# A convolution kernel's seam: the last step's spectra kept on chip, the other rows reloaded a step earlier, the inverse products moved ahead of the mixing's transposes

## The chip, the cores and the metric

One core of a Trainium2 chip runs the kernel; the others are idle. The metric is the device time of one execution in microseconds: 677.84 us, the median of 3 runs (677.25 to 677.91). TensorE is written PE, VectorE DVE, ScalarE ACT, GpSimd POOL, and SP is the engine that only issues transfers.

## The reference

Two halves, each modulated by a condition vector `c` (shift, scale and gate are 512 wide each), over a sequence of 2048 rows of 512 channels:

```python
# half A: a long convolution per channel, through the Fourier transform
P = jnp.exp(logdA[:, :, None] * l[None, None, :])
K = jnp.einsum("dn,dnl,dn->dl", Cc, P, dB).real
Kf, Uf = rfft2(pad(K)), rfft2(pad(u))
y = irfft2(Uf * Kf)[..., :L] + u * Dskip
x = x + ga * y                                   # u = layernorm(x) * (1 + ca) + sa
# half B: on h = layernorm(x) * (1 + cb) + sb
m  = gelu(layernorm(h) @ w1)                     # then shifted by +1, -1, +2, -2 rows by quarter
x1 = h + shifted(m) @ w2
x  = x + gb * (x1 + gelu(layernorm(x1) @ w3) @ w4)
```

## The kernel before, in words

All is fp32; half B's products are split into high and low parts and done as three products. Up to about 205 us the kernel builds the convolution's taps and the input's first transform. Then come the spectra, and then half B.

**The spectral loop** (`steps`, 16 of them) covers two channel halves `jh` of 256 channels, each in 8 steps `kc`. A step does, on PE, `spectrum_k` (64 products, taps, from the buffer `VK[jh]` with the tables `T2` and `T3`) and `spectrum_u` (the input, with the table `TU`); on ACT the copies `us`; on DVE `multiply`, which leaves `zc0` and `zc1`. `back` turns these with the table `Gm` (tile name FK): four products of 64 columns into two banks `pz`, which ACT evicts to `z`. POOL stores `z` to the DRAM scratch `ZT[jh]`; in the very last step SP and ACT each store half. The loop is skewed: `back` of step n-1 stands in pass n, `spectrum_u` of step n+1 too.

**The inverse** needs, for each output block, rows of all 8 steps, in another order: `load_inv` reads `ZT[jh]` back in 8 chunks of 128 rows by 4 x 256, and `inv_half(jh, g, i)` does 8 products of 32 columns (`FI` times a chunk) into a bank; DVE adds it to `X2`, the sequence in row blocks (tile name KX). `g` is one of four groups of four blocks, `i` a pair in it. The first half's inverse (`jh` 0) runs in passes 14 and 15 and around the end of the loop. The second half's can only start when the last step's rows have been stored and loaded.

**Behind the seam** the mixing runs through groups 7, 0, 1, 2, ... of 256 rows: `first_stats`, `mix_mod1`, `mix_mod2` (DVE with POOL for the roots), `mix_norm` (ACT), `transposed` (PE, 8 transposes to `pT0` and `pT1`), `parts_of` (ACT makes `nh`, DVE the residual `nl`), `mix_half` (PE products with `W1h` and `W1l`, ACT's gelu `go`, a store to `GD`). The closures `a31`, `a00`, `a30`, `a01`, `a10`, `a11`, `a20` and `a21` are DVE's adds of the second half's eight inverse tiles. `keep(n)` issues n products that nobody reads, into `pT0`.

**What sets the order.** Everything here is in a manual schedule: each engine runs its instructions in the order of the program text, and only waits on semaphores. Tiles that share memory make an instruction wait for the last user. Transfers from SP and ACT take turns on eight semaphores; a transfer waits until the eighth before it has landed. So an instruction that is late delays all that stands behind it on its engine.

Of the kernel before, what the change touches and what calls it, by code (L numbers as in the profile page):

```python
# [24 lines left out]
NXC = 16 * NX0 + 64 * NX1  # L25


def shape_constants():
# [19 lines left out]
    Gm = np.tile(np.concatenate([cs, cs], 1), (2, 1))  # L48
    sg = np.array([1.0, -1.0])[:, None]
    th = 2 * np.pi * (k1[:, None, None, None] + .5) * (sg * be[:, None, None] + 64 * q) / 4096  # L50
    FI = np.stack([np.cos(th), -sg * np.sin(th), -np.sin(th), -sg * np.cos(th)]) * (2 / 4096)
    eye = np.eye(16)
# [18 lines left out]
    for e in range(16):  # L71
# [9 lines left out]
        FI=FI.reshape(128, 32 * 64), C0=C0, C1=C1, CE=CE, PA=PA.reshape(128, 512), PB=PB.reshape(128, 2048), ID=np.eye(128)).items()}  # L81
# [28 lines left out]
def dram(t, off, ap):  # L110
    return bass.AP(tensor=t.tensor, offset=t.offset + off, ap=ap)


def body(ctx, tc, A):
# [534 lines left out]
    T3 = s2.tile([128, 32, 64], F32, name="T3", bufs=1)  # L649

# [37 lines left out]
    def back(jh, kc):  # L688
        zc = zcs.pop((jh, kc))
        z = s2.tile([128, 4, 256], F32, name="z", bufs=3)  # L690
        o = [psa.tile([128, 2, 256], F32, name="pz") for kk in range(2)]
        for n in range(2):
            for kk in range(2):
                r = slice(kk * 64, kk * 64 + 64)
                T.matmul(o[kk][n * 64:n * 64 + 64], Gm[r, n], zc[n][r], start=True, stop=True, skip_group_check=True)  # L695

        def store(q, a, b):
            for n in range(2):
                q.dma_start(dram(ZT[jh], n * 16384 + (kc * 4 + a) * 256, [[32768, 32], [8192, 2], [1, (b - a) * 256]]),
                            z[n * 64:n * 64 + 64, a:b].rearrange("p k d -> p (k d)"))  # L700

        last = (jh, kc) == (1, 7)
        for kk in range(2):
            act(z[:, 2 * kk:2 * kk + 2], o[kk])
            if last:
                store((Y, S)[kk], 2 * kk, 2 * kk + 2)
        if not last:
            store(P, 0, 4)

    def load_inv(jh, k, i=None, q=Y):  # L710
        if (jh, k) not in zis:
            zis[jh, k] = block() if jh or k in (1, 2, 5, 6) else zip_.tile([128, 4, 256], F32, name="zi")
        a, n = (0, 4) if i is None else (2 * i, 2)
        q.dma_start(zis[jh, k][:, a:a + n], dram(ZT[jh], (k * 4 + a) * 32768, [[256, 128], [32768, n], [1, 256]]))

    def load_x(g):
        P.dma_start(X2[:, g * 4:g * 4 + 4].rearrange("p b d -> p (b d)"), A["x"][g])

    def inv_half(jh, g, i, pl, name):
        p = pl.tile([128, 2, 256], F32, name=name)  # L720
        for e in range(2):
            b = g * 4 + i * 2 + e
            for bp, (c, sg) in enumerate(((31 - b, 1), (15 - b, 1), (b, 0), (16 + b, 0))):
                T.matmul(p[bp * 32:bp * 32 + 32, e], FI[:, c, sg], zis[jh, c // 4][:, c % 4],
                         start=True, stop=True, skip_group_check=True)
        x = X2[:, g * 4 + i * 2:g * 4 + i * 2 + 2, jh * 256:jh * 256 + 256]
        return lambda: V.tensor_add(x, p, x)
# [365 lines left out]
    with tc.manual_schedule():  # L1093
# [13 lines left out]
        for n, st in enumerate(steps):  # L1107
# [26 lines left out]
            if n == 14:  # L1134
                inverse(0, 0)
                for b in range(4):
                    half_stat(b, 0)
                w2r = [block().rearrange("p (a c) b -> p a (c b)", a=2) for i in range(2)]
                for i in range(2):
                    Y.dma_start(w2r[i], A["w2"][256 * i:256 * i + 256].rearrange("(a p) n -> p a n", p=128))  # L1140
# [5 lines left out]
        back(*steps[15])  # L1146
# [18 lines left out]
        for k, i in ((3, 1), (0, 0)):  # L1165
            load_inv(1, k, i, Y)
            load_inv(1, k + 4, i, Y)
        for k, i in ((3, 0), (0, 1)):
            load_inv(1, k, i)
            load_inv(1, k + 4, i)  # L1170
        for f in i1:
            f()
# [22 lines left out]
        mix_norm(7)  # L1195
        first_stats(0)
# [6 lines left out]
        a10 = inv_half(1, 1, 0, psy, "py")  # L1203
        a11 = inv_half(1, 1, 1, psy, "py")
# [10 lines left out]
        a20 = inv_half(1, 2, 0, psy, "py")  # L1215
# [7 lines left out]
        a21 = inv_half(1, 2, 1, psy, "py")  # L1223
# [85 lines left out]
```

## Time and profile before

| what | us |
|---|---|
| median of 3 runs | 677.84 |
| profiled execution, its own time | 677.99 |
| its span | 676.2 |
| PE busy (matmuls) | 633.9, 94% |
| DVE busy | 495.7, 73% |
| ACT busy | 333.4, 49% |
| POOL busy | 114.7, 17% |

Times in the rows count from the start of the span. A row of the timeline gives the start, the duration, the engine, the line, the operation, output and inputs and, in brackets, how long the engine was idle before and what ended that. Lines are those of the kernel before; most copies of ACT stand under L122, its helper's line. PE records an fp32 product twice. A busy share is an average over stages with different limits, so the stretch around 285 to 350 us is read by itself.

### The profile page before, as it was taken

How to read it: one execution, taken by the hardware profiler on the slowest of the kernel's cores; microseconds unless marked ns; L12 is line 12 of the kernel's file. 1: busy time of each engine (PE TensorE's matmuls, PEld its weight loads, DVE VectorE, ACT ScalarE, POOL GpSimd, SP SyncE). 2: the span in 40 equal slices, each digit the busy share in tenths (PEclk: the TensorE clock that was granted, in tenths of full speed). 3: DMA queues.
4: the chain of work that ended last, by engine and by line, in shares of the span. 5: the costliest groups of instructions: out<-in, count | busy, mean ns of one | idle time of the engine just before them, and what ended most of it. 6: DMA issues, size and time to landing. Idle time of an engine off the chain costs nothing.

```text
span 676.2 us, 16864 instructions
## 1 busy us (share of the span) xinstructions
PE 633.9 (94%) x7195; PEld 507.1 (75%) x7195; DVE 495.7 (73%) x793; ACT 333.4 (49%) x507; POOL 114.7 (17%) x228
## 2 busy tenths in 40 slices
PE   2899999999999998967999999999999999999996
PEld 1456556665568886635889899898998989898895
DVE  7888999999996898897989777454674445363622
ACT  5878998898884666632446334032141213122121
POOL 2102212212206133203843002010010000000000
PEclk9998999999999999998999999999999999999999
DMA  9602274642828999976386010110100201010001
GB/s 323 271 2 75 75 230 107 196 130 76 300 65 276 323 350 380 363 215 195 111 270 235 1 64 1 53 43 16 53 26 30 65 18 46 1 63 1 1 32 31
DMA packets 49924, 86.43 MB, mean 128 GB/s; under 512 B 4533, under 2 KB 38329, under 8 KB 47257
## 3 DMA queue, kind: packets, MB, share of 16 engines
q1 hardware_dynamic: 44904, 60.97, 28.3%
q0 software_dynamic: 4624, 23.86, 9.6%
q8 instruction: 56, 0.92, 0.6%
q10 hardware_dynamic: 320, 0.52, 0.3%
q14 instruction: 20, 0.16, 0.1%
HBM read 59.12 MB, written 32.90 MB: 136 GB/s over the span
## 4 chain that ended last, share of the span: by engine, by line
PE 72%; DMA 5%; DVE 4%; ACT 2%; issue 2%; POOL 1%; SPq 1%; ACTq 0%; DVEq 0%; POOLq 0%
PE xx L440 7%; PE pm L834 7%; PE pm L832 7%; PE pm L831 7%; PE pa L950 6%; PE pa L951 6%; PE pa L958 6%; PE pk L673 4%; PE kp L490 3%; DMA w4l<-Dw 2%; PE pz L695 2%; PE pk L643 2%; PE ph L889 2%; PE ph L888 2%; PE ph L891 2%
## 5 line engine op out<-in xcount | busy, mean ns | idle before, releaser
L122 ACT ACTIVATE gh<-pm 128x512 fp32r<-128x512 f32 (+1 forms) x48 | 26.9, 560 | 199.0 <-PE pm L834 199.0
L831 PE MATMUL pm<-nh,w3h 128*128 128x256 f32 (+1 forms) x352 | 85.6, 278 | 0.0
L832 PE MATMUL pm<-nh,w3l 128*128 128x256 f32 (+1 forms) x352 | 85.5, 278 | 0.1
L942 DVE TENSOR_TENSOR gl<-gf,gh 128x512 fp32r<-128x512 f32 (+1 forms) x48 | 30.8, 643 | 68.0 <-ACT gf L122 68.0
L950 PE MATMUL pa<-w4h,gh 128*128 128x512 f32 (+1 forms) x176 | 69.6, 395 | 0.0
L951 PE MATMUL pa<-w4l,gh 128*128 128x512 f32 (+1 forms) x176 | 68.9, 392 | 0.0
L832 PEld LDWEIGHTS pm<-nh,w3l 128*128 128x128 f32 (+1 forms) x352 | 65.2, 185 | 2.1 <-DVE w3l L751 0.5
L831 PEld LDWEIGHTS pm<-nh,w3h 128*128 128x128 f32 (+1 forms) x352 | 65.3, 185 | 1.4
L758 POOL TENSOR_TENSOR rs<-mv,eps_t 128x1 f32<-128x1 f32 (+1 forms) x39 | 10.9, 281 | 272.7 <-DVE mv L764 256.0
L834 PE MATMUL pm<-nl,w3h 128*128 128x256 f32 (+1 forms) x352 | 54.7, 277 | 0.1
L441 PE MATMUL xx<-MG,ON 64*128 64x512 f32 x160 | 48.1, 397 | 0.0
L440 PE MATMUL xx<-MG,ON 64*128 64x512 f32 x160 | 48.1, 396 | 0.0
L958 PE MATMUL pa<-w4h,gl 128*128 128x512 f32 (+1 forms) x176 | 48.0, 390 | 0.0
L834 PEld LDWEIGHTS pm<-nl,w3h 128*128 128x128 f32 (+1 forms) x352 | 46.5, 185 | 0.3 <-DVE nl L804 0.3
L894 DVE TENSOR_TENSOR h<-h,ph 128x512 f32<-128x512 f32 x16 | 11.0, 687 | 44.8 <-PE ph L891 44.8
L458 DVE SCALAR_TENSOR_TENSOR e<-tr,p 128x512 f32<-128x512 f32 x64 | 41.1, 684 | 2.5 <-ACT tr L122 2.2
L490 PEld LDWEIGHTS kp<-e,e 128*32 128x32 f32 x2048 | 30.0, 110 | 13.1 <-issue 7.6
L467 DVE TENSOR_TENSOR e<-tr,p 128x1024 f32<-128x1024 f32 x32 | 39.0, 1219 | 1.1 <-ACT tr L122 1.1
L468 DVE TENSOR_TENSOR e<-tr,m 128x1024 f32<-128x1024 f32 x32 | 39.0, 1219 | 0.0
L122 ACT ACTIVATE p<-xx 128x1024 f32<-128x1024 f32 (+1 forms) x40 | 37.5, 980 | 2.1 <-PE xx L258 0.7
L958 PEld LDWEIGHTS pa<-w4h,gl 128*128 128x128 f32 (+1 forms) x176 | 33.0, 188 | 7.2
L673 PE MATMUL pk<-VK,xu 64*64 64x128 f32 x768 | 36.0, 270 | 1.8 <-issue 1.8
(250 smaller groups left out, 1706.2 us busy)
## 6 DMA issues: line engine op xcount, KB each, us to landing
VU<-vs SPq DMA_DIRECT2D x64, 128.0 KB, 3.0
ld<-VU SPq DMA_DIRECT2D x16, 512.0 KB, 9.2
ZT<-z POOLq DMA_DIRECT2D x30, 256.0 KB, 6.2
Dw<-in_w POOLq DMA_DIRECT2D x8, 688.0 KB, 4.6
xu<-in_u SPq DMA_DIRECT2D x4, 1024.0 KB, 8.3
KX<-in_x POOLq DMA_DIRECT2D x4, 1024.0 KB, 8.8
ld<-ZT SPq DMA_DIRECT2D x8, 512.0 KB, 5.5
win<-GD SPq DMA_DIRECT2D x32, 128.0 KB, 2.4
```

The source lines that it names most:

```text
L122: return S.activation(out, in_, f, bias=bias, scale=scale)
L440: T.matmul(x[:, :512], la, ma, start=(i == 0), stop=(i == len(ops) - 1))
L441: T.matmul(x[:, 512:], lb, mb, start=(i == 0), stop=(i == len(ops) - 1))
L458: V.scalar_tensor_tensor(e0[:, 1, a], tr[:, 1, 0], 1.0 - 2.0 * a, mg[:, a], op0=OP.mult, op1=OP.mult)
L490: T.matmul(kp[32 * j:32 * j + 32, (k % 2) * 4 + g], e1[:, r, d], e0[:, r, :, d * 32:d * 32 + 32], start=(r == 0), stop=(r == 1), skip_grou ...
L673: T.matmul(p[gh][kk * 64:kk * 64 + 64, i, ro], w, VK[jh][rows, ri * 32 + k1].rearrange("p j g -> p (j g)"), start=(ri == 0), stop=(ri == 1 ...
L831: T.matmul(p, wh[:, k, c], hi[k], start=(k == 0), stop=False)
L832: T.matmul(p, wl[:, k, c], hi[k], start=False, stop=False)
L834: T.matmul(p, wh[:, k, c], lo[k], start=False, stop=(k == 3))
L950: T.matmul(acc[i], gh[:m, e, s], W4h[:m, f], start=(f == 0), stop=False)
L951: T.matmul(acc[i], gh[:m, e, s], W4l[:m, f], start=False, stop=False)
L958: T.matmul(acc[i], gl[:m, e, s], W4h[:m, f], start=False, stop=(f == 10))
```

## The change

**Last step.** `back_late` replaces `back` for step 15. It uses a table `GB` and 16 products of 32 columns by 256, and ACT evicts the two banks into `ZL`, in memory of `T2[1]`. Nothing of step 15 goes to DRAM. Each output block then takes two sets of products: 8 with `FL` times `ZL` (`inv_last`), and 8 with `FI` times the reloaded rows (`main`), summed in the same bank. `FL` holds, for each of eight sets of columns, a table in which all rows but those of that set are zero; `late_tables` writes it in passes 12 and 13, with eight ACT copies that scale by a column of zeros and ones, into memory of `T2[0]`. The small table comes by one more load (`FL`, 256 KB) in pass 10, into a part of `TU` that is no longer read.

**The other rows.** `ZT`'s rows are sorted by step, so the last 16 of each chunk are step 15's, and a load reads 112 of 128. All twelve loads go to SP, in one block, into memory of `VK[1]`; they wait for step 14's store and for step 15's `spectrum_k`. The first half of W2 is loaded in pass 13 into another part of `TU`.

**The order.** The products of all eight tiles stand before group 7's transposes, in four pairs: (3,1) and (0,0), (3,0) and (0,1), (1,0) and (1,1), (2,0) and (2,1). The pool `psy` has four banks for two. `keep` is defined but not called.

On ACT, in passes 12 to 15 of the loop. First before, then in the change; the tile `xu` is `T2`'s memory, `wm` is `TU`'s:

```order
L122 ACTIVATE z<-pz 128x512 x2
L122 ACTIVATE us<-pk_4289 128x512
L122 ACTIVATE us<-pk_4290 128x512
L122 ACTIVATE us<-pk_4289 128x512
L122 ACTIVATE w1h<-w1l 128x512 x2
L122 ACTIVATE z<-pz 128x512 x2
L122 ACTIVATE us<-pk_4360 128x512
```

```order
L134 ACTIVATE xu<-wm 128x4x64 x4
L134 ACTIVATE z<-pz 128x512 x2
L134 ACTIVATE us<-pk_4294 128x512
L134 ACTIVATE us<-pk_4295 128x512
L134 ACTIVATE us<-pk_4294 128x512
L134 ACTIVATE w1h<-w1l 128x512 x2
L134 ACTIVATE xu<-wm 128x4x64 x4
L134 ACTIVATE z<-pz 128x512 x2
L134 ACTIVATE us<-pk_4370 128x512
```

Four table copies stand ahead of the eviction `z` of step 12, four more ahead of that of step 13, behind the copies for W1.

On PE, from the transform of step 15 (`zc`) to group 7's transposes, before and then in the change, which begins with the last of the new transform's eight rows:

```order
L695 MATMUL pz<-zc_4437,FK 64x512 x2
L695 MATMUL pz<-zc_4438,FK 64x512 x2
L724 MATMUL py<-ld,FI 32x256 x16
L1163 MATMUL pT_4596<-w1h 128x512 x6
L724 MATMUL py<-ld,FI 32x256 x16
L724 MATMUL pm<-ld,FI 32x256 x16
L1163 MATMUL pT_4648<-w1h 128x512 x14
L796 MATMUL pT_4704<-ident,h_4663 128x128 x4
L796 MATMUL pT_4705<-ident,h_4663 128x128 x4
L724 MATMUL py<-ld,FI 32x256 x16
```

```order
L730 MATMUL pz<-zc_4446,wm 32x256 x2
L772 MATMUL py<-ld,FI 32x256 x16
L756 MATMUL py<-xu 32x256 x16
L762 MATMUL py<-VK_3051,FI 32x256 x16
L756 MATMUL pm<-xu 32x256 x16
L762 MATMUL pm<-VK_3051,FI 32x256 x16
L756 MATMUL py<-xu 32x256 x16
L762 MATMUL py<-VK_3051,FI 32x256 x16
L756 MATMUL py<-xu 32x256 x16
L762 MATMUL py<-VK_3051,FI 32x256 x16
L844 MATMUL pT_4789<-ident,h_4680 128x128 x4
L844 MATMUL pT_4790<-ident,h_4680 128x128 x4
```

Two tiles of the second half (the last row before) moved from behind the transposes to before them, two more from behind the mixing of groups 7 and 0, and each tile has twice the products.

On SP, from the last input loads to the first mixing store, before and in the change:

```order
L633 DMA ld<-VU 128x4x256 x12
L714 DMA zi<-ZT_61 128x4x256 x4
L714 DMA ld<-ZT_61 128x4x256 x4
L1140 DMA ld<-in_w 128x2x512 x2
L699 DMA ZT_62<-z 32x2x512 x2
L714 DMA ld<-ZT_62 128x2x256 x8
L714 DMA ld<-ZT_62 128x4x256 x4
L846 DMA GD<-go 128x2x256
```

```order
L645 DMA ld<-VU 128x4x256 x11
L1177 DMA wm<-in_FL 128x512
L645 DMA ld<-VU 128x4x256
L742 DMA zi<-ZT_61 128x4x256 x4
L742 DMA ld<-ZT_61 128x4x256 x4
L1181 DMA wm<-in_w 128x2x512
L1193 DMA ld<-in_w 128x2x512
L742 DMA VK_3051<-ZT_62 112x2x256 x8
L742 DMA VK_3051<-ZT_62 112x4x256 x4
L894 DMA GD<-go 128x2x256
```

The last step's stores are gone, and one table load is new. The twelve loads stand in the same place, with nothing but W2 ahead of them.

The diff, without the tables' constants:

```diff
-        def store(q, a, b):
-            for n in range(2):
-                q.dma_start(dram(ZT[jh], n * 16384 + (kc * 4 + a) * 256, [[32768, 32], [8192, 2], [1, (b - a) * 256]]),
-                            z[n * 64:n * 64 + 64, a:b].rearrange("p k d -> p (k d)"))
-
-        last = (jh, kc) == (1, 7)
         for kk in range(2):
             act(z[:, 2 * kk:2 * kk + 2], o[kk])
-            if last:
-                store((Y, S)[kk], 2 * kk, 2 * kk + 2)
-        if not last:
-            store(P, 0, 4)
+        for n in range(2):
+            P.dma_start(dram(ZT[jh], kc * 4096 + n * 2048, [[32768, 32], [1024, 2], [1, 1024]]),
+                        z[n * 64:n * 64 + 64].rearrange("p k d -> p (k d)"))
+
+    def late_tables(i):
+        for c in range(4 * i, 4 * i + 4):
+            act(FL[:, :, c], FC, AF.Identity, scale=which[:, c:c + 1])
+
+    def back_late():
+        zc = zcs.pop(steps[15])
+        o = [psa.tile([128, 2, 256], F32, name="pz") for m in range(2)]
+        for m in range(4):
+            for n in range(2):
+                for i in range(2):
+                    r = slice((2 * n + i) * 32, (2 * n + i) * 32 + 32)
+                    T.matmul(o[m // 2][r, m % 2], GB[:, m], zc[n][:, i], start=True, stop=True, skip_group_check=True)
+        for m in range(0, 4, 2):
+            act(ZL[:, m:m + 2], o[m // 2])
...
+            if jh:
+                zis[jh, k] = VK[1].rearrange("p a b c -> p (a b c)")[:, k * 1024:k * 1024 + 1024].rearrange("p (n d) -> p n d", n=4)
...
+        r = 112 if jh else 128
+        q.dma_start(zis[jh, k][:r, a:a + n], dram(ZT[jh], (k * 4 + a) * 32768, [[256, r], [32768, n], [1, 256]]))
...
+    def inv_last(g, i, pl, name):
+        p = pl.tile([128, 2, 256], F32, name=name)
+        b0 = g * 4 + i * 2
+        x = X2[:, b0:b0 + 2, 256:512]
+        for e in range(2):
+            for bp, (c, sg) in enumerate(parts_at(b0 + e)):
+                m, s = LATE_AT[c]
+                T.matmul(p[bp * 32:bp * 32 + 32, e], FL[:, m, s, sg * 32:sg * 32 + 32], ZL[:, m], start=(e == 0), stop=False,
+                         skip_group_check=True)
+
+        def main():
+            for e in range(2):
+                for bp, (c, sg) in enumerate(parts_at(b0 + e)):
+                    T.matmul(p[bp * 32:bp * 32 + 32, e], FI[:112, c, sg], zis[1, c // 4][:112, c % 4],
+                             start=False, stop=True, skip_group_check=True)
+            return lambda: V.tensor_add(x, p, x)
+        return main
...
+            if n == 10:
+                Y.dma_start(TU[:, 0:8], A["FL"].rearrange("p (a b) -> p a b", a=8))
+            if n in (12, 13):
+                late_tables(n - 12)
+            if n == 13:
+                Y.dma_start(w2r[0], A["w2"][0:256].rearrange("(a p) n -> p a n", p=128))
...
-        back(*steps[15])
+        back_late()
...
-        psy = a2.enter_context(tp("psy", 2, space=PSUM, side="right"))
+        psy = a2.enter_context(tp("psy", 4, space=PSUM, side="right"))
...
+        for k in (1, 5, 2, 6):
+            load_inv(1, k)
...
-        for k in (1, 2):
-            load_inv(1, k)
-            load_inv(1, k + 4)
-        keep(6)
-        inv_half(1, 3, 1, psy, "py")()
+
+        def pair(*gi, pl, name):
+            fs = [inv_last(g, i, pl, name) for g, i in gi]
+            return [f() for f in fs]
+
+        a31, a00 = pair((3, 1), (0, 0), pl=psy, name="py")
+        a31()
         first_stats(7)
-        a00 = inv_half(1, 0, 0, psy, "py")
-        a30 = inv_half(1, 3, 0, psw, "pm")
-        a01 = inv_half(1, 0, 1, psw, "pm")
-        keep(14)
+        a30, a01 = pair((3, 0), (0, 1), pl=psw, name="pm")
...
         mix_norm(7)
+        a10, a11 = pair((1, 0), (1, 1), pl=psy, name="py")
+        a20, a21 = pair((2, 0), (2, 1), pl=psy, name="py")
         first_stats(0)
...
-        a10 = inv_half(1, 1, 0, psy, "py")
-        a11 = inv_half(1, 1, 1, psy, "py")
...
-        a20 = inv_half(1, 2, 0, psy, "py")
...
-        a21 = inv_half(1, 2, 1, psy, "py")
```

More of the change, by code (lines that the diff above doesn't have):

```diff
@@ L25 @@
 NXC = 16 * NX0 + 64 * NX1
+LATE = [[s + v + u for s in (14 - 2 * m, 2 * m) for u in (0, 16) for v in (0, 1)] for m in range(4)]
+LATE_AT = {c: (m, i) for m in range(4) for i, c in enumerate(LATE[m])}
 def shape_constants():
@@ L48, in shape_constants @@
     Gm = np.tile(np.concatenate([cs, cs], 1), (2, 1))
+    GB = np.zeros((2, 64, 4, 2, 8, 2))
+    for m in range(4):
+        for kk in range(2):
+            GB[kk, :, m, kk] = cs.reshape(64, 32, 2)[:, LATE[m]]
     sg = np.array([1.0, -1.0])[:, None]
@@ L51, in shape_constants @@
     FI = np.stack([np.cos(th), -sg * np.sin(th), -np.sin(th), -sg * np.cos(th)]) * (2 / 4096)
+    F7 = FI.reshape(2, 2, 8, 2, 2, 32, 64)[:, :, 7]
+    FC = np.stack([F7[..., LATE[m], :] for m in range(4)], 4)
+    FC = FC.transpose(0, 3, 2, 5, 1, 4, 6).reshape(128, 256)
+    FI = FI.reshape(4, 8, 4, 32, 2, 32).transpose(1, 0, 2, 3, 4, 5).reshape(128, 32, 2, 32)
+    which = np.tile(np.repeat(np.eye(8), 2, 0), (8, 1))
+    FL = np.concatenate([FC, GB.reshape(128, 128), which, np.zeros((128, 120))], 1)
     eye = np.eye(16)
@@ L707, in back @@
[L707 to L708 removed]
+        for n in range(2):
[7 more added lines that the diff above has]
+        o = [psa.tile([128, 2, 256], F32, name="pz") for m in range(2)]
+        for m in range(4):
+            for n in range(2):
[4 more added lines that the diff above has]
+            act(ZL[:, m:m + 2], o[m // 2])
```

24 lines of the change are left out of this document (13 added, 11 removed).

## The prediction

> **What bounds the kernel now.** I read the busy time by stage first, then the chain of waits around the seam that the diff touches, then single rows there. Columns of the first view: stretch, length, busy time (and rows) of PE, weight load, DVE, ACT and POOL, granted clock, DMA share, GB/s.
>
> ```profile
> 263.00:291.00 28.00, 25.46 (x577) 19.52 (x573) 25.23 (x44) 18.16 (x36) 7.15 (x13) 1.00 1.03 365
> 291.00:300.00 9.00, 7.24 (x98) 3.62 (x90) 8.41 (x18) 3.59 (x7) 1.07 (x2) 1.00 0.54 144
> 300.00:312.00 12.00, 6.24 (x68) 3.56 (x69) 8.04 (x16) 0.00 (x0) 1.79 (x4) 0.72 0.86 264
> 318.90:347.70 28.80, 27.20 (x239) 23.82 (x232) 27.02 (x55) 12.21 (x19) 19.11 (x52) 1.00 0.46 146
> 372.00:672.00 300.00, 298.84 (x1919) 269.79 (x1917) 159.36 (x264) 75.81 (x141) 18.10 (x47) 1.00 0.09 29
> ```
>
> From 372 us on PE works 298.84 of 300 us: nothing there gets shorter, and a microsecond won before it is a microsecond of the whole. The hole is 300 to 312, with PE busy for 6.24 of 12 us. Between 318.9 and 347.7 DVE (27.02 of 28.8) is as full as PE, so work taken from PE alone buys little there.
>
> ```profile
> 291.33 3.61 issue
> 296.71 2.66 DMA ZT<-z
> 301.09 4.54 DMA ld<-ZT
> 317.81 1.86 PE py L724 x32
> ```
>
> The chain names the hole: the last spectrum goes out (2.66 us) and comes back (4.54 us) before the inverse products can start. Then 1.86 us of inverse products stand between the first transposes and the mixing.
>
> ```profile
> 301.77 2.49 DVE L1180 TENSOR_TENSOR w2l<-ld,w2h 128x512 fp32r<-128x512 f32 x4
> 305.76 3.64 PE L724 MATMUL py<-ld,FI 128*32 128x256 f32 x32 [7.53 <-DMA ld<-ZT]
> 307.75 0.69 DVE L727 TENSOR_TENSOR KX<-py,KX 128x512 f32<-128x512 f32 x1 [3.49 <-PE py L724]
> 314.61 0.66 DVE L727 TENSOR_TENSOR KX<-py,KX 128x512 f32<-128x512 f32 x1
> 315.75 0.44 PE L796 MATMUL pT<-ident,h 128*128 128x128 f32 x2 [1.18 <-ACT h L122]
> 317.74 1.93 PE L724 MATMUL py<-ld,FI 128*32 128x256 f32 x32
> 318.90 1.28 DVE L804 TENSOR_TENSOR nl<-pT,nh 128x512 fp32r<-128x512 f32 x2
> 319.61 0.39 PE L831 MATMUL pm<-nh,w1h 128*128 128x256 f32 x1
> ```
>
> PE waits 7.53 us for that load, but DVE only 3.49 us: it has the W2 residuals until 304.26. So 3.49 us, not 7.53, is the most that this wait can give while DVE's order stays, and its order does stay. I follow three marks: the first add (DVE, 307.75), the second add (314.61) and the residual nl of group 7 (318.90), from which DVE runs almost unbroken to 347.7.
>
> **The change part by part.** *The loads leave sooner.* Their last store is now that of step 14.
>
> ```profile
> 291.61 1.07 POOL L699 DMA_DIRECT2D ZT<-z  x2 [4.65 <-ACT z L122]
> ZT<-z POOLq DMA_DIRECT2D x2, 256.0 KB, 3.5
> 299.57 5.30 SPq L714 DMA_DIRECT2D ld<-ZT  x10
> ```
>
> The second half of that store is issued near 292.1 and lands 3.5 us later, at 295.6; with the 0.2 us that SP takes, the first load leaves at 295.8, 3.8 us before today's 299.57. Today the fourth load lands at 305.63 (301.09 + 4.54); so it would be 301.85, less what the shift below takes. The 112 rows for 128 I count as nothing (an eighth of the bytes; the bound is 0.5 us sooner, and DVE covers it).
>
> *Table copies in front of an eviction.* Eight ACT copies of 128x256 elements with a scale operand are new, four in step 12, four in step 13.
>
> ```profile
> L122 ACT ACTIVATE w2h<-ld 128x512 fp32r<-128x512 f32 x4 | 2.2, 618 | 1.4 <-DVE KX L727 1.4
> L122 ACT ACTIVATE KX<-hpi 128x1 f32<-128x1 f32 x1 | 0.2, 202 | 0.0
> L122 ACT ACTIVATE h<-h,nm,rs 128x512 f32<-128x512 f32 x16 | 12.9, 814 | 27.9 <-POOL nm L821 27.8
> 280.47 1.08 ACT L122 ACTIVATE z<-pz 128x512 f32<-128x512 f32 x2 [2.37 <-PE pz L695]
> 282.87 1.18 ACT L122 ACTIVATE w1h<-w1l 128x512 fp32r<-128x512 f32 x2
> 284.52 1.09 ACT L122 ACTIVATE z<-pz 128x512 f32<-128x512 f32 x2 [0.46 <-PE pz L695]
> 285.28 2.13 PE L724 MATMUL pz<-zi,FI 128*32 128x256 f32 x32
> 286.87 1.29 DVE L727 TENSOR_TENSOR KX<-pz,KX 128x512 f32<-128x512 f32 x2
> ```
>
> 618 ns for 512 elements and 202 for one make 0.81 ns per element, 409 ns for 256. Two operands (scale, bias) cost 814 - 618 = 196 ns, so one costs 98: 507 ns. Neighbours overlap by 0.1 us (two evictions of 595 ns take 1.09), which leaves 0.41 each, 1.7 us for four. The four of step 12 fit into the 2.37 us that ACT idles before 280.47. The four of step 13 start at 284.05 with 0.46 us idle ahead, so the eviction of 284.52 comes 1.1 to 1.2 us later. Behind it wait the products at 285.28, which write the banks that it empties, and behind them in PE's order the last spectrum products and the step-14 transform; DVE's add at 286.87 waits for the former. DVE's row there shows no wait, so I allow it 0.2 us of slack: the last step slides by **0.9 us**, and the store and loads with it. Bounds: nothing, if ACT is early enough, and 2.2 us at h's full 814 ns per copy. I take 0.9, nearest the two rows of the copy's own kind.
>
> *The last step's transform.* Sixteen products of 32 columns replace four of 64.
>
> ```profile
> 290.11 1.93 PE L724 MATMUL pk<-zi,FI 128*32 128x256 f32 x32
> 291.86 1.91 PE L724 MATMUL pk<-ld,FI 128*32 128x256 f32 x32
> 293.70 1.09 PE L695 MATMUL pz<-zc,FK 64*64 64x512 f32 x8
> 294.72 1.93 PE L724 MATMUL py<-ld,FI 128*32 128x256 f32 x32
> 295.86 0.69 DVE L727 TENSOR_TENSOR KX<-py,KX 128x512 f32<-128x512 f32 x1 [0.34 <-PE py L724]
> ```
>
> A product is recorded twice, so x32 is 16: 1.75 us from start to start (290.11 to 291.86). The old transform holds PE for 1.02 us (293.70 to 294.72), so what follows slides by **0.73 us**, DVE's add at 295.86 with it, since DVE is waiting there. The two ACT copies of the result take the place of the old two; the ACT stores fall away.
>
> *First mark.* DVE is through at 304.26 + 0.9 + 0.73 = 305.9. The loads are there at 301.85 + 0.9 = 302.75, PE has the sum 1.1 us later. So DVE is the later one: the add starts at 305.9, **1.85 us** sooner. If DVE's cover were gone, PE's date would allow 2 us more.
>
> *Products ahead of the transposes.* All eight tiles are now finished before group 7 is transposed: 64 main products and 64 from the late table, eight units of 16. The first unit needs no load and runs in the hole. Seven units follow the loads: 302.75 + 7 x 1.75 = 315.0. But the last tile takes the bank that the second add empties: 314.61 + 0.66 - 1.85 = 313.4, and from there half a unit and the last main unit, 2.6 us: **316.05**. The tile to be transposed would have been ready from 313.9 (315.75 - 1.85). So PE is late, not the data. What stood behind them goes away: no 1.93 us at 317.74, no 8 products later on twice.
>
> ```profile
> 342.78 1.03 PE L796 MATMUL pT<-ident,h 128*128 128x128 f32 x8
> 344.17 0.39 PE L831 MATMUL pm<-nh,w1h 128*128 128x256 f32 x1 [0.35 <-ACT nh L122]
> ```
>
> Undisturbed, mixing starts 1.4 us after the transposes; the residual needs only their first half and one copy, about 1.2 us. So mixing starts at 317.45 instead of 319.61, nl at 317.25 instead of 318.90. The smaller gain, **1.65 us**, is what DVE carries on to 347.7; the 2.1 us of inverse products that PE no longer does up to there lie beside DVE's work and count as nothing (if DVE had room, they would be worth up to 1 us). The removed filler products (20) ran while PE waited; they cost nothing, unless the clock falls, below. The new 256 KB table load and the earlier W2 load go into a stretch whose queues are full (DMA share 1.03 from 263 to 291), but the loads they precede have microseconds to spare: nothing, bound 0.7 us.
>
> Sum: the profiled execution took 677.99 us (span 676.2 and 1.8 around it), the median is 677.84; 677.84 - 1.65 = **676.2 us**.
>
> [...] The filler's job is the clock.
>
> ```profile
> 298.30:302.50 4.20, 0.00 (x0) 0.00 (x0) 4.20 (x10) 1.29 (x3) 0.00 (x0) 1.00 0.57 177
> 302.50:305.70 3.20, 0.00 (x0) 0.00 (x0) 1.76 (x3) 0.00 (x0) 0.00 (x0) 0.50 1.00 279
> 305.70:309.30 3.60, 3.54 (x36) 1.90 (x40) 1.48 (x4) 0.00 (x0) 0.00 (x1) 0.50 1.07 354
> ```
>
> PE stops at 298.3, the clock is half from 302.5, and stays half for 3.6 us of work. In the change PE pauses from about 300.1 to 302.75, 2.7 us. If that were enough to halve one such window, 1.6 us of PE time would be lost, 1.0 of it in the wait for the bank: 676.8 us. [...]
>
> **Rivals.** *Larger gain*: the step-13 copies cost the last step nothing, and both marks come 0.9 us sooner: 675.3 us. For it: ACT is busy for 18.16 of 28 us in that stretch. Against it: the eviction has only 0.46 us of idle time ahead.
>
> *Eaten up*: the copies cost 814 ns each, the last step slides by 2.2 us, and the bank is free 1.3 us later: transposes at 317.35, nl at 318.55, 0.35 us gained, 677.5 us. A halved window or full queues (0.7 us) end between this and the forecast. For it: a strided output and a scale operand, of which no row shows the pair.
>
> *Slower, the loads are not sooner*: the step-14 store lands as those before it did.
>
> ```profile
> ZT<-z POOLq DMA_DIRECT2D x4, 256.0 KB, 6.6
> ```
>
> That is the median from 281 to 287. Then 3.1 us come on top: main products from 305.85, PE has paused for almost 6 us, so the clock is half as it was (1.7 us lost): 305.85 + 12.25 + 1.7 = 319.8, nl at 321.0, 2.1 us late: 679.9 us. It decides from transposes at 317.7: a store that takes 6.2 us, or 4.5 with the halved clock. For it: the store's addresses change (its two runs per column lie side by side now), and the whole queue of inverse products stands ahead of the transposes. Against it: the queues empty after 291 (DMA share 0.54), which is why the last store took 3.5. By this rival the change does not do what it says.
>
> **How the numbers follow.** Forecast 0.46 (its own range 675.5 to 676.9), larger gain 0.12, eaten up 0.29, slower 0.13. A measurement of this kernel can tell about 0.2%, 1.36 us, from no change, so "faster" ends at 676.48: three quarters of the forecast's chance and the larger gain, 0.47; a quarter of the forecast and the eaten case, 0.40; slower 0.13. The range 674.9 to 678.4 takes in the larger gain, the eaten case and the start of the slower one; it leaves out the rest of that and a DVE that finds room.
>
> **What would show it.** Right: the first load issued near 296.7 and DVE's add at 305.9 with no idle time ahead; the eviction of step 13 delayed by about 1.1 us behind four copies near 0.5 us; transposes at 316, the last late products before them waiting for DVE; mixing at 317.4; clock 1.0 throughout. Wrong: DVE idle again before the first add (then the loads were late), transposes later than 317.7, half clock after 302, or table copies off 0.5 us.

## The result and the profile after

The change takes 683.62 us (median of 6 runs, 681.01 to 685.2), the kernel before 678.54 us beside it (677.25 to 680.08): a ratio of 1.0068, with an interval of 1.004 to 1.0095. It is slower by 5.1 us (by the medians; 4.6 by the ratio), where 676.2 was forecast. The profiled execution took 685.2 us with a span of 683.4, so it lies 1.6 us above the median.

The views that answer to those shown of before. First the busy time by stage of the change (columns as in the prediction):

```profile
300.00:312.00 12.00, 8.18 (x104) 3.77 (x96) 11.64 (x25) 0.00 (x0) 2.52 (x5) 0.72 0.97 231
306.00:314.00 8.00, 8.00 (x113) 3.97 (x108) 7.54 (x16) 0.61 (x1) 4.28 (x10) 0.72 1.10 222
318.90:347.70 28.80, 25.41 (x217) 21.48 (x210) 21.33 (x44) 10.53 (x17) 15.71 (x45) 0.91 0.32 106
372.00:672.00 300.00, 299.80 (x1936) 271.37 (x1936) 163.69 (x272) 80.59 (x150) 20.52 (x51) 1.00 0.09 30
```

The old hole, 300 to 312, is partly filled (PE 8.18 us for 6.24, DVE 11.64 for 8.04). But DVE, nearly full from 318.9 to 347.7 before (27.02 us), is now busy for only 21.33 of 28.8. And in the middle of the reload (306 to 314) the DMA engines have a busy share of 1.10 and move 222 GB/s. (The share is the sum of the packets' times over the time of 16 engines, so it can pass 1.) Before, the reload has this row:

```profile
304.00:310.00 6.00, 4.24 (x48) 2.34 (x52) 2.08 (x6) 0.00 (x0) 0.62 (x2) 0.56 1.07 353
```

About the same busy share, 1.07, but 353 GB/s. The chain of waits of the change now holds one long piece in this place:

```profile
304.92 11.46 DMA VK<-ZT
```

It is the last of the twelve loads, 11.46 us on its way. Who waits for it stands in the timeline of PE, and DVE's rows show what it costs:

```profile
297.04 1.91 PE L772 MATMUL py<-ld,FI 128*32 128x256 f32 x32
304.49 3.64 PE L762 MATMUL py<-VK,FI 112*32 112x256 f32 x32 [3.82 <-DMA VK<-ZT]
310.90 1.90 PE L762 MATMUL pm<-VK,FI 112*32 112x256 f32 x32
316.43 2.87 PE L762 MATMUL py<-VK,FI 112*32 112x256 f32 x32 [1.90 <-DMA VK<-ZT]
319.05 2.73 PE L756 MATMUL py<-xu 128*32 128x256 f32 x32
323.43 1.09 PE L844 MATMUL pT<-ident,h 128*128 128x128 f32 x8
```

```profile
306.50 0.69 DVE L764 TENSOR_TENSOR KX<-py,KX 128x512 f32<-128x512 f32 x1
313.12 0.66 DVE L764 TENSOR_TENSOR KX<-py,KX 128x512 f32<-128x512 f32 x1
324.76 1.29 DVE L852 TENSOR_TENSOR nl<-pT,nh 128x512 fp32r<-128x512 f32 x2 [7.27 <-ACT nh L134]
332.59 1.29 DVE L852 TENSOR_TENSOR nl<-pT,nh 128x512 fp32r<-128x512 f32 x2 [0.29 <-ACT nh L134]
```

The first two adds of DVE come where they were forecast, once this execution's late start is taken off (see below). Then the third pair's main products (316.43) wait for the last four loads, the fourth pair follows, partly at half clock (its late products take 2.73 us for 1.91), and only then, at 323.43, come the transposes (forecast 316.05). DVE stands idle for 7.27 us ahead of nl, which comes at 324.76 instead of 318.90.

### The profile page after: what moved, and what is told of

It reads as the page before. It is cut to its first block, busy times and chain, and to the rows that moved or that the text cites. A ratio compares the mean times of both kernels' runs of the same rounds, so it can differ in the third digit from the quotient of the medians.

```text
span 683.4 us, 17120 instructions
## 1 busy us (share of the span) xinstructions
PE 641.0 (94%) x7327; PEld 511.7 (75%) x7327; DVE 496.3 (73%) x793; ACT 336.3 (49%) x515; POOL 113.6 (17%) x228
## 4 chain that ended last, share of the span: by engine, by line
PE 75%; DMA 5%; DVE 4%; ACT 3%; issue 2%; SPq 1%; POOL 1%; DVEq 0%; ACTq 0%; POOLq 0%
PE xx L452 8%; PE pm L882 7%; PE pm L880 7%; PE pm L879 7%; PE pa L998 6%; PE pa L999 6%; PE pa L1006 6%; PE pk L690 4%; PE kp L502 4%; PE pz L712 2%; DMA w4l<-Dw 2%; PE pu L430 2%; PE pk L655 2%; PE ph L937 2%; PE ph L936 2%; PE ph L939 2%
## 5 line engine op out<-in xcount | busy, mean ns | idle before, releaser
L690 PEld LDWEIGHTS pk<-VK,xu 64*64 64x64 f32 x768 | 33.0, 133 | 6.3 <-issue 5.5
```

What stands on the lines that cost most here:

```text
L690: T.matmul(p[gh][kk * 64:kk * 64 + 64, i, ro], w, VK[jh][rows, ri * 32 + k1].rearrange("p j g -> p (j g)"), start=(ri == 0), stop=(ri == 1 ...
```

## The experiments

Three questions were open: why the reload is slow, what its slowness costs, and which mark the end follows. All times of a row below come from one profiled execution, whose own time is in the column "profiled"; medians and ratios come from the runs beside the kernel before. "nl 7", "nl 0", "nl 1" are DVE's residuals of groups 7, 0 and 1, "sixth nl" is the last one before PE is full.

| kernel | median us | before, beside it | ratio (interval) | profiled | eviction 12 | nl 7 | nl 0 | nl 1 | sixth nl |
|---|---|---|---|---|---|---|---|---|---|
| before | | | | 677.99 | 280.47 | 318.90 (38.43) | 326.73 (46.26) | 336.86 | 363.88 (83.41) |
| the change | 683.62 | 678.54 | 1.0068 (1.004 to 1.0095) | 685.20 | 281.50 | 324.76 (43.26) | 332.59 (51.09) | 342.72 | 370.85 (89.35) |
| e1 128 rows | 679.00 | 678.90 | 1.0014 (0.9994 to 1.0034) | 678.45 | 279.26 | 318.86 (39.60) | 326.71 (47.45) | 336.86 | 363.88 (84.62) |
| e3 before, rows sorted | 679.31 | 678.90 | 1.0004 (0.9992 to 1.0016) | 678.07 | 279.73 | 318.95 (39.22) | 326.79 (47.06) | 336.93 | 363.95 (84.22) |
| e4 two pairs behind | 680.66 | 678.90 | 1.0024 (1.0008 to 1.0041) | 678.75 | 279.92 | 315.73 (35.81) | 326.93 (47.01) | 337.39 | 364.44 (84.52) |
| e6 e5 without filler | 680.93 | 678.53 | 1.0041 (1.0017 to 1.0065) | 681.06 | 280.29 | 318.53 (38.24) | 328.94 (48.65) | 338.81 | 366.68 (86.39) |
| e9 spread | 678.27 | 678.66 | 0.9980 (0.9961 to 0.9999) | 678.27 | 280.75 | 316.55 (35.80) | 325.89 (45.14) | 336.61 | 363.67 (82.92) |
| e10 spread, 112 rows | 678.31 | 678.66 | 0.9991 (0.9976 to 1.0006) | 678.56 | 281.05 | 316.84 (35.79) | 326.17 (45.12) | 336.91 | 363.97 (82.92) |
| e11 e9 without filler | 677.52 | 678.66 | 0.9974 (0.9957 to 0.9992) | 677.06 | 279.21 | 315.01 (35.80) | 324.73 (45.52) | 335.46 | 362.55 (83.34) |
| e12 spread finer | 676.94 | 679.11 | 0.9976 (0.9960 to 0.9991) | 675.09 | 279.26 | 315.06 (35.80) | 323.87 (44.61) | 333.75 | 360.80 (81.54) |

The executions do not reach the seam at the same time. "Eviction 12" is the start of ACT's eviction of step 12, for which ACT waits on PE in each of them, so that the table copies do not move it. It lies between 279.21 and 281.50. The numbers in brackets count from it, and marks of two kernels are compared by them below. A difference under 1 us says little even so: e3 does the work of the kernel before, and its marks lie 0.8 us later by this count.

The theories of the first four runs: A, a load of 112 rows is slow wherever it is; B, the new place is slow (rows sorted by step, or the taps' memory); C, the order costs the time and not the transfer.

### e1: 128 rows again

```diff
-        r = 112 if jh else 128
+        r = 128
...
+        fill = T2[0].rearrange("p a b -> p (a b)")
+        for n in range(2):
+            P.dma_start(dram(ZT[1], 7 * 4096 + n * 2048, [[32768, 32], [1024, 2], [1, 1024]]), fill[n * 64:n * 64 + 64, :1024])
```

> The change with one thing undone: the twelve loads of the second half read 128 rows instead of 112. The products still use 112, so nothing is left out. The sixteen extra rows hold a filler that one store writes at about 190 us, where the queues are nearly idle. Theory A (a transfer of 112 rows moves slowly, whatever the place): the reload, about 230 one-KB packets per us in the change against 355 before, goes back to about 350 although there are 14% more bytes; all twelve loads have landed by about 311 us instead of 316; the products of the third pair wait for no load; transposes near 316.5, and 677 to 678.5 us against 683.6 for the change and 678.5 for the kernel before. Theory B (the new place is slow: rows sorted by step in DRAM, or the taps' memory as the goal): the rate stays at 230, the last loads land 2 us later than in the change, 685 to 686 us. Theory C (the order, four pairs ahead of the transposes, costs the time, not the transfer): the rate may go back, but transposes come later than 319 and the time stays above 681 us.

```profile
304.00:310.00 6.00, 6.00 (x98) 3.34 (x92) 5.62 (x13) 0.00 (x0) 2.83 (x5) 0.82 1.05 339
```

```profile
301.96 2.92 PE L762 MATMUL py<-VK,FI 112*32 112x256 f32 x32 [3.51 <-DMA VK<-ZT]
312.22 1.93 PE L762 MATMUL py<-VK,FI 112*32 112x256 f32 x32 [1.46 <-DMA VK<-ZT]
317.54 1.09 PE L844 MATMUL pT<-ident,h 128*128 128x128 f32 x8
```

The first row is by stage, the others are PE's. Sixteen more rows, and the reload runs at 339 GB/s. The last loads are there at 312.2 instead of 316.4 (2.0 us sooner, counted from the eviction), transposes at 317.54, 679.0 us, no longer distinguishable from the kernel before. Against the kernel beside it the change was 5.1 us slower, e1 0.1 (by its interval between 0.4 us faster and 2.3 slower): the row count carries most of the loss in this order. A was right in kind and off by up to 1 us: pair 3 still waits, for 1.46 us, the transposes were said for 316.5, and 679.0 lies above its 677 to 678.5. Counted from the eviction, e1's marks are still 1.2 us later than those of the kernel before.

### e2, e3, e8: which property of the load

e2 gives the kernel before loads and products of 112 rows, e8 of 96 (each leaves out the other rows of the second half); e3 gives it the sorted rows.

```diff
 # e2 (e8: 96)
+        r = 112 if jh else 128
-        q.dma_start(zis[jh, k][:, a:a + n], dram(ZT[jh], (k * 4 + a) * 32768, [[256, 128], [32768, n], [1, 256]]))
+        q.dma_start(zis[jh, k][:r, a:a + n], dram(ZT[jh], (k * 4 + a) * 32768, [[256, r], [32768, n], [1, 256]]))
 # e3
-                q.dma_start(dram(ZT[jh], n * 16384 + (kc * 4 + a) * 256, [[32768, 32], [8192, 2], [1, (b - a) * 256]]),
+                q.dma_start(dram(ZT[jh], kc * 4096 + n * 2048 + a * 256, [[32768, 32], [1024, 2], [1, (b - a) * 256]]),
```

> The kernel before with one thing done: the loads of the second half read 112 rows of 128 (old order of the rows, old buffers), and the products of that half use 112 rows. Left out: 16 of 128 rows of each chunk, so the second half's inverse lacks an eighth of its terms; the products cost PE the same time. Theory A: the reload falls from 355 packets per us to about 230, the fourth 448... here four loads of 224 KB land 1 to 2 us later than before's four of 256 KB, the first products start after 306.5 us instead of 305.76, and the whole takes 679 to 681 us. Theory B: nothing but fewer bytes; the rate stays near 350, 678.0 to 678.5 us. Theory C says nothing of this run beyond B's number.

> The kernel before with one thing done: the rows of the scratch are sorted by step as in the change (both halves), with the inverse table permuted to match; loads of 128 rows into the old buffers, all products as before, nothing left out. Theory A: no difference, 678.5 us within 0.7, the reload at 350 packets per us. Theory B, if it is the sorting: the reload at about 230 per us, the first products 2 us later, 680 us or more; if it is the taps' memory, no difference here either, and then e1 must have stayed slow.

> e2 with 96 rows instead of 112 (left out: 32 of 128 rows of each chunk of the second half). It asks which counts of rows are slow. [...]

By stage, e2:

```profile
304.00:310.00 6.00, 3.98 (x36) 1.80 (x40) 1.90 (x6) 0.00 (x0) 0.74 (x3) 0.50 1.14 233
```

e3:

```profile
304.00:310.00 6.00, 4.19 (x52) 2.36 (x56) 1.83 (x5) 0.00 (x0) 0.57 (x2) 0.60 1.07 352
```

e8:

```profile
304.00:310.00 6.00, 3.54 (x36) 1.93 (x40) 2.34 (x6) 0.00 (x0) 0.00 (x0) 0.50 1.11 251
```

In the old kernel, with the old rows and buffers, 112 rows bring the rate from 353 to 233 GB/s, 96 rows to 251; the sorted layout leaves it at 352. So A holds and B falls. That 112 is an odd multiple of 16, the number of DMA engines, is not the reason, since 96, 6 times 16, is slow too. But the times of e2 and e3 are those of the kernel before: 678.81 us (0.9998, 0.9984 to 1.0012) and 679.31 us (1.0004, 0.9992 to 1.0016), and e8's one time is 678.75. A's 679 to 681 us for e2 was wrong: a slow reload alone costs nothing that these runs can tell (at most 0.8 us by e2's interval), although nl 0 comes later in e2's one profile, at 328.11. It costs where work stands behind it.

### e4: two pairs back behind the transposes

```diff
         mix_norm(7)
-        a10, a11 = pair((1, 0), (1, 1), pl=psy, name="py")
-        a20, a21 = pair((2, 0), (2, 1), pl=psy, name="py")
...
         mix_mod2(0, 1)
+        a10, a11 = pair((1, 0), (1, 1), pl=psy, name="py")
...
         a11()
+        a20, a21 = pair((2, 0), (2, 1), pl=psy, name="py")
```

> The change with only its order undone for half of the tiles: the third and the fourth pair of inverse tiles stand behind the transposes of group 7 and behind those of group 0, as their tiles did before; the loads stay at 112 rows. Theories A and B: group 7's transposes no longer stand behind the loads that land at 316.4; they come when the data is there, about 315 to 316, nl at about 317.5; the 7 us of products of the two pairs now lie in the stretch up to 347.7 us where PE had 1.6 us to spare, and 3.5 us of that were there before; the third pair still waits for its loads until about 316.5 but that is hidden: 679 to 681 us. Theory C: the same, or better than the kernel before (below 678). If the time stays at 683 or above, the transposes were not what the products held up.

ACT's eviction of step 12 and DVE's residuals, then PE:

```profile
279.92 1.09 ACT L134 ACTIVATE z<-pz 128x512 f32<-128x512 f32 x2 [0.80 <-PE pz L712]
315.73 1.28 DVE L852 TENSOR_TENSOR nl<-pT,nh 128x512 fp32r<-128x512 f32 x2
326.93 1.29 DVE L852 TENSOR_TENSOR nl<-pT,nh 128x512 fp32r<-128x512 f32 x2 [3.75 <-ACT nh L134]
```

```profile
312.59 0.44 PE L844 MATMUL pT<-ident,h 128*128 128x128 f32 x2 [2.64 <-ACT h L134]
315.06 3.09 PE L756 MATMUL py<-xu 128*32 128x256 f32 x32
317.98 1.90 PE L762 MATMUL py<-VK,FI 112*32 112x256 f32 x32
325.61 1.03 PE L844 MATMUL pT<-ident,h 128*128 128x128 f32 x8
```

680.66 us, as A said, with the slow loads: some 3 us of the 5.1 are back. But nl 7 comes 2.6 us sooner than in the kernel before (counted from the eviction; A had expected less), and this kernel is still 1.8 us slower. The next residual, nl 0, is no sooner than before (0.75 us later): DVE waits 3.75 us for it, because PE puts pair 3 (315.06 to 319.81) between the two groups' transposes. nl 7 is not the mark that the end follows.

### e5, e6, e7: the late products in the pause

With 128 rows, the late products of three pairs fill PE's pause; pair 4 follows the transposes of group 7. e6 leaves the filler out. e7 is e5 with the table copies in passes 11 and 12.

```diff
+        f1 = late((3, 1), (0, 0), pl=psy, name="py")
+        f2 = late((3, 0), (0, 1), pl=psw, name="pm")
+        f3 = late((1, 0), (1, 1), pl=psy, name="py")
+        a31, a00 = [f() for f in f1]
...
+        a30, a01 = [f() for f in f2]
...
+        keep(24)
+        a10, a11 = [f() for f in f3]
...
         mix_mod2(0, 1)
+        a20, a21 = [f() for f in late((2, 0), (2, 1), pl=psy, name="py")]
```

> e1 (128 rows) with another order on PE: the late-table products of the first three pairs stand together ahead of all products that need a load; then the main products of pairs 1 and 2, 24 filler products, the main products of pair 3, the transposes of group 7, and only then pair 4. Theory D (what e1 still lacks is the halved clock after the pause, 1.6 us, and the wait of pairs 3 and 4 ahead of the transposes): no pause from 298 to 302, granted clock 1.0 from 296 to 316, main products of pair 1 from about 302 at 1.75 us per unit, transposes near 314 (e1: 317.54), the residual nl near 315.2 (e1: 318.86, before: 318.90); 3.5 us of products behind the transposes, as many as before; 3.2 to 3.6 us less than the kernel before, about 675.3 us. Theory E (the stretch to 347.7 us is as full on DVE and PE as the date of nl can make it): nl comes sooner but the end does not, 677.5 to 678.5 us, as in e4, where nl came at 315.73 and the time was 680.7.

> e5 without its 24 filler products: PE stands still from about 305.5 to 311 us, until the loads of pair 3 have landed. Theory D: the clock is half again from about 309.5 to 316, the main products of pair 3 take 3.5 us for 1.75, the transposes 2 us for 1, nl 1 to 2.5 us later than in e5, and the end as much: 676.5 to 678 us. Theory E: no difference to e5 beyond 0.5 us.

> e5 with the eight table copies on ACT in the passes 11 (three) and 12 (five) instead of 12 and 13, and their load in pass 9 instead of 10. In the change the four copies of pass 13 push the eviction of that pass by 1.0 us (5.05 us from the eviction before it instead of 4.05), and half of that is left at the last step. Expected if the copies are the cause: that interval is 4.05 to 4.2 again, the last step's eviction comes 14.5 instead of 15.0 us after that of pass 12, and everything behind it 0.5 us sooner, 0.3 to 0.6 us less than e5. If the full queues are the cause of the delay instead, nothing changes.

The times are 681.06, 680.93 and 681.39 us, each slower than the kernel before (e5's ratio 1.0032, 1.0013 to 1.0051; e7's 1.0033, 1.0015 to 1.0051). e5 missed both of its forecasts and e6 that of D; that e6 takes as long as e5 is what E said. e7 is not faster than e5. e5, PE (this execution took 685.28 us, 4.2 above its median):

```profile
309.01 3.27 PE L762 MATMUL pm<-VK,FI 112*32 112x256 f32 x32 [2.19 <-DMA VK<-ZT]
312.20 6.05 PE L1219 MATMUL pT<-w1h 128*128 128x512 f32 x24
320.05 1.09 PE L844 MATMUL pT<-ident,h 128*128 128x128 f32 x8
```

e6, PE:

```profile
313.22 3.64 PE L762 MATMUL py<-VK,FI 112*32 112x256 f32 x32 [4.59 <-DMA VK<-ZT]
318.23 1.93 PE L756 MATMUL py<-xu 128*32 128x256 f32 x32
327.62 1.04 PE L844 MATMUL pT<-ident,h 128*128 128x128 f32 x8
```

Two mistakes in the design of e5: 24 filler products take 6.05 us, and are themselves what the transposes wait for; and pair 4 is 3.5 us of PE between the two transposes, so nl 0 comes 10.4 us behind nl 7 (e6: 318.53 to 328.94) instead of 7.8. Counted from the eviction, e6 has nl 7 1.4 us sooner than e1, but nl 0 1.2 us and the sixth nl 1.8 us later, and it is e6 that is slower than the kernel before. On the copies e7 is not conclusive: in its passes 11 to 13 waits fall in other places than in e5.

### e9, e10, e11, e12: nothing between the transposes that is not needed there

Theory F: the end follows nl 0, so PE's work between group 7's and group 0's transposes has to be short. In e9 the main products of pair 3 stand in the middle of group 7's mixing, pair 4 behind group 0's transposes. e10 is e9 with 112 rows, e11 e9 without its 16 filler products, e12 moves single tiles.

```diff
 # e9
+        keep(16)
...
         mix_half(7, hl, 0)
+        a10, a11 = [f() for f in f3]
...
         hl = parts_of(transposed(mh.pop(0)[0]))
+        f4 = late((2, 0), (2, 1), pl=psy, name="py")
...
         mix_half(0, hl, 0)
+        a20, a21 = [f() for f in f4]
 # e12 against e9
-        keep(16)
+        g20 = late((2, 0), pl=psy, name="py")
+        keep(10)
...
-        a10, a11 = [f() for f in f3]
+        a10 = f3[0]()
...
-        f4 = late((2, 0), (2, 1), pl=psy, name="py")
+        g21 = late((2, 1), pl=psy, name="py")
+        a11 = f3[1]()
...
-        a20, a21 = [f() for f in f4]
+        a20 = g20[0]()
...
         hl = parts_of(transposed(mh.pop(1)[0]))
+        a21 = g21[0]()
```

> The 128 rows and the late products ahead as in e5, but with no products of pairs 3 and 4 between group 7's transposes and its mixing: main products of pairs 1 and 2, 16 filler products, transposes of group 7, first half of its mixing, main products of pair 3, second half, transposes of group 0, late products of pair 4, first half of group 0's mixing, main products of pair 4, second half. Theory F (what the end follows is not nl of group 7 but nl of group 0, which waits for PE's work between the two transposes: 326.7 us in the kernel before, in e1 and in e4 alike, although nl of group 7 came between 315.7 and 318.9): transposes of group 7 near 313, those of group 0 near 322, nl of group 0 near 323.5, 3 us sooner than before, and the end with it: 675.5 to 676.3 us. Theory E (DVE, or the transfers around 350 to 370 us, hold the end anyway): nl of group 0 is sooner, but the marks behind it are not, and the time stays at 678 or above.

> e9 with the change's 112 rows and without the filler store: nothing but the order differs from the change. The reload runs at 220 to 240 packets per us and lands at about 315 us. Theory F: only the main products of pair 3 wait for it, 1 to 2 us in the middle of group 7's mixing; nl of group 0 near 325, still 1.5 us ahead of the kernel before, 677 us; the order alone is then worth 6 us against the change. If the slow transfer is the whole story, the time stays near 683.

> e9 without its 16 filler products. PE stands still for about 4 us before the transposes of group 7. If the clock halves after that (it did in e6 after 4.6 us), the transposes and the first 3 us of the mixing take twice as long: nl of group 0 1.5 to 2 us later than in e9, 677.2 to 678 us. If the pause is too short, no difference to e9.

> e9 with single tiles instead of pairs in the places behind the loads: the late products of tile (2,0) and 10 filler products before group 7's transposes (its bank is free there), the main products of tile (1,0) alone in the middle of group 7's mixing, those of (1,1) and the late products of (2,1) behind group 0's transposes, the main products of (2,0) in the middle of group 0's mixing, those of (2,1) behind group 1's transposes. Theory F in full (between two residuals nl the later of PE's work and DVE's sets the pace): PE's stretch from group 7's to group 0's transposes loses 0.9 us against e9 (nl of 7 to nl of 0: 8.4 us instead of 9.3), PE's next one is 9.6 us instead of 10.7, so DVE's 10.1 holds (nl of 0 to nl of 1: 10.1 instead of 10.7), the next one stays at DVE's 8.0. Together 1.5 us less than e9 and 2 us less than the kernel before: 676.2 to 677.0 us. Theory E (something further on holds the end): these three distances come as said and the time still stays at 678.

e10, with the change's own 112 rows, takes 678.31 us, no longer distinguishable from the kernel before: the order alone (with its filler) takes back the 5.1 us. Its reload and the two places that use it last:

```profile
304.00:310.00 6.00, 3.87 (x65) 1.95 (x65) 5.72 (x12) 0.00 (x0) 2.22 (x4) 1.00 1.13 247
```

```profile
314.02 0.41 PE L844 MATMUL pT<-ident,h 128*128 128x128 f32 x2
320.04 1.93 PE L762 MATMUL py<-VK,FI 112*32 112x256 f32 x32
```

247 GB/s, slow as in the change (244 in the same 6 us), and the products of pair 3 wait for nothing. e9 with its fast reload is no better (678.27). Either undoing alone is enough, as far as these runs can tell: the loss needs the slow reload and the products in the way together. e9's gain was forecast at 3 us and came out near the edge of what can be told, since nl 0 was at 325.89 and not at 323.5 (1.1 us sooner than in the kernel before, counted from the eviction): the main products of pair 3 cost 1.75 us there, and the transposes waited for h until 314.60. e11's 677.52 us lies inside its forecast by luck: without the filler the clock halved, as said (310.15 to 316.98), but nl 0 comes only 0.4 us later than in e9 by the count from the eviction, not 1.5 to 2, and the time is not above that of e9; the two intervals overlap.

e12's eviction of step 12 (ACT) and its steps (DVE):

```profile
279.26 1.09 ACT L134 ACTIVATE z<-pz 128x512 f32<-128x512 f32 x2 [0.53 <-PE pz L712]
315.06 1.28 DVE L852 TENSOR_TENSOR nl<-pT,nh 128x512 fp32r<-128x512 f32 x2
323.87 1.29 DVE L852 TENSOR_TENSOR nl<-pT,nh 128x512 fp32r<-128x512 f32 x2 [1.27 <-ACT nh L134]
333.75 1.29 DVE L852 TENSOR_TENSOR nl<-pT,nh 128x512 fp32r<-128x512 f32 x2
```

The distances are 8.81 and 9.88 us (expected 8.4 and 10.1; e9 had 9.34 and 10.72), and the end follows: 676.94 us. This is the size of gain that the change was forecast to have (1.6 us by the ratio, 2.2 by the medians), and 6 to 7 us less than the change, with the same last-step transform and tables and with loads of 128 rows.

These runs also settle which mark counts. Counted from the eviction, nl 7 comes at 35.8 us in e4, e9, e10, e11 and e12 alike, 2.6 us sooner than in the kernel before. nl 0 comes at 47.0, 45.1, 45.1, 45.5 and 44.6 us, and the sixth nl ranks them in the same order. In the medians e4, the last at nl 0, is the only one of the five that is slower than the kernel before; the differences among the other four are too small for these runs.

## Why the prediction was wrong, point by point

**Right.** The loads left when forecast: 296.7 was said, they were issued from 297.84 in an execution that was already 1.03 us late at the eviction of step 12 (281.50 for 280.47, a mark that lies between 279.2 and 281.5 in the profiles of the kernels with the same table copies). On the same footing, with the 1.03 taken off: first add 305.5 (said 305.9), second add 312.1 (said 312.8). The transform holds PE for 1.73 us (said 1.75). The table copies take 0.43 us each (said 0.41):

```profile
281.50 1.09 ACT L134 ACTIVATE z<-pz 128x512 f32<-128x512 f32 x2 [0.81 <-PE pz L712]
284.94 1.72 ACT L134 ACTIVATE xu<-wm 128x256 f32<-128x256 f32 x4
286.54 1.10 ACT L134 ACTIVATE z<-pz 128x512 f32<-128x512 f32 x2
296.47 0.60 ACT L134 ACTIVATE xu<-pz 128x512 f32<-128x512 f32 x1 [3.43 <-issue]
```

The eviction of step 13 comes 5.04 us behind that of step 12 (4.05 before), so 1.0 us late (said 1.1 to 1.2); of that 0.5 is left at the last step (14.97 us from eviction 12 to eviction 15, before 14.47), where 0.9 was said. So the date of the loads came out partly by luck: step 14's store slid by 0.7 us instead of 0.9 (POOL issues it at 293.33, before at 291.61), and from its issue to the first load it took 4.5 us, 0.3 more than said.

**The step that failed: "the 112 rows for 128 I count as nothing".** The bound given was 0.5 us on the good side. Measured, the rows cost over a third of the rate (353 to 222 GB/s), and the twelve loads take 18.5 us from the first issue to the last landing. The prediction followed the first four loads only; the last four, for pairs 3 and 4, were not in the sum at all. In its sum the main products of pair 3 would start at 309.75 (302.75 and four units); they started at 316.43, 5.65 us later on the same footing, after PE had waited 1.90 us for the last load. Even at the rate of 128 rows (e1) the last loads are there at 312.2 in an execution that is 1.21 us early at the eviction, so at 313.4 on the footing of before; three units of 1.75 behind them make 318.7, not 316.05. So the forecast was out of reach in this order with 128 rows too.

**"Seven units follow the loads" put them in front of the transposes as if only PE's time counted.** That order made every load a condition for the mixing; in the kernel before only the first eight were.

**The mark.** That the gain at nl "is what DVE carries on to 347.7" is true of nl 0, not of nl 7. e4 wins 2.6 us at nl 7 and none at nl 0. From nl 0 to the sixth nl it is 36.9 to 37.8 us in every kernel of the table but the change (38.3). The break-even point, transposes at 317.7, was not tested by e1: its transposes come at 317.54, which is 318.75 on the footing of before, and its time cannot be told from that of before.

**The clock.** The sum took the clock as full over a pause of 2.7 us, which no run shows; if it was not, 676.8 us were said. The change showed a pause of 3.82 us and half clock from 303.63 to 310.45; this would have mattered little alone, as far as can be argued, since the last loads came later. A second half-clock window, 317.28 to 320.69, fell on the products that the transposes wait for: from 316.43 to 323.43 the three units took 7.0 us instead of 5.25.

**The rivals.** "The loads are not sooner" came nearest in kind (transposes 319.8, 679.9 us), but by a late store, which did not happen. A slow reload was not among them. Of the signs of being wrong, transposes later than 317.7 and half clock after 302 came; DVE was not idle before the first add, so the first loads were not late.

**Left open.** Why a load of 112 or 96 rows is slow. And in this profile 4.8 of the 7.2 us of longer span are there at nl 0 beyond the common 1.03, and 1.3 more come behind it: nl 1 to the next is 8.85 us for 7.95, behind a half-clock window. Such a window is there in e5 and e7 too (from 343.58 and 339.70), not in e1, e4, e9 and e12. The part of the median that it makes was not measured.

## What to carry to other kernels

Fewer bytes were not a faster load here (in the kernel before, 353 GB/s with 128 rows, 233 with 112 in e2): before a transfer's shape is changed, look for its new shape in a trace, and follow the last transfer of the group, not the first. When products are moved ahead of an engine's next step, list every load that the step now waits for. And check which of several marks the end follows: hold the nearest one fixed and see whether the next one moves.

## What was not expected of the hardware

**Rows.** From 304 to 310 us, loads of 1-KB rows ran at 339, 352 and 353 GB/s with 128 rows (e1, e3, the kernel before), at 233, 244 and 247 with 112 (e2, the change, e10) and at 251 with 96 (e8), all with the DMA engines at a busy share of 1.03 to 1.14. From 306 to 312 us, e5's 128 rows ran at 341 and e4's 112 at 219, at shares of 1.05 and 1.14. How the rows are split among the 16 engines, and why the loads with fewer rows ran at lower rates, was not shown by any run here.

**Clock.** The granted clock changes in steps of 3.41 us: from 262 to 372 us, the half-clock stretches of the 14 profiles last one to four such windows. In the change, three times, the window before and the half one:

```profile
300.22:303.63 3.41, 0.45 (x12) 0.00 (x0) 3.41 (x9) 0.00 (x0) 0.00 (x0) 1.00 0.76 203
303.63:307.04 3.41, 2.55 (x24) 1.19 (x28) 3.40 (x6) 0.00 (x0) 0.00 (x0) 0.50 0.96 257
313.87:317.28 3.41, 1.51 (x31) 0.67 (x24) 3.34 (x8) 1.15 (x2) 2.05 (x7) 1.00 0.37 74
317.28:320.69 3.41, 3.41 (x37) 1.74 (x32) 0.21 (x1) 0.00 (x0) 0.00 (x0) 0.50 0.00 0
341.18:344.59 3.41, 1.82 (x13) 1.41 (x12) 3.34 (x7) 0.00 (x0) 2.77 (x9) 1.00 0.53 184
344.59:348.00 3.41, 3.41 (x18) 3.41 (x17) 3.27 (x9) 0.86 (x2) 1.51 (x6) 0.50 0.99 305
```

PE was busy for 0.45, 1.51 and 1.82 of the 3.41 us, and the next window was half. No window was idle throughout; the longest wait in the second was 1.90 us. Over the 14 profiles, from 262 to 372 us, all 14 full-clock windows with PE busy for up to 44% were followed by half clock, none of those with 55% or more, and of those between 48 and 53% three of six. So in these profiles the half clock went with PE's busy share of the window before, with the border between 44 and 55%. If the 2.7 us of pause that the prediction forecast fall into one window, PE's share there is at most 21% (0.71 of 3.41 us, an estimate), so that pause could have halved the clock too.
